# A gated mix of attention and a channel MLP: other buffers for the MLP's finished tiles, chunk sums copied in two halves, and one chunk's last half batch moved up a turn

## The chip, the cores and the metric

The kernel runs on one core of a Trainium2 chip. A core has a matrix engine (TensorE, PE in the profile, with its weight loads as PEld), a vector engine (DVE), a scalar engine (ACT), GpSimd (POOL), a sync engine (SP) that mainly issues DMAs, and sixteen DMA engines. Every engine works through its own list of instructions in order; an instruction waits until the semaphores it names are high enough, and what stands behind it on the same engine waits too.

The metric is the device time of one execution in microseconds (us), as the median of several runs. Lower is better.

## The reference

```python
x = A_x                                    # 1 x 2048 x 448, float32
g = sigmoid((x * gate_w).sum(-1, keepdims=True))
qkv = x @ wqkv                             # 16 heads of 28
p = softmax(q @ k.T * 28 ** -0.5)          # per head, 2048 x 2048
a = (p @ v) @ wo
y = layernorm(x)
b = gelu(y @ w1 + b1) @ w2 + b2            # 448 -> 1792 -> 448
return g * a + (1 - g) * b
```

All tensors are float32. The kernel splits each operand of a precise product into a high and a low part in a rounded format and adds three products of the parts; the product of probabilities and values is a plain float32 one.

## The kernel before, in words

**Stages.** The kernel has a head (the projections to q, k and v, until about 130 us), the MLP (until about 451 us) and the attention (until the end, 1082 us). Rows are worked on in four chunks of 512 (`CH`), heads in four groups of four; 16 pairs of group and chunk, `n` from 0 to 15, make up the attention.

**Row maxima.** The softmax needs the maximum of each row of scores before it can take exponentials. A cheap single product per tile gives scores good enough for that: `RowMax.one` (L207) issues one matmul into a PSUM bank and one DVE `reduce_max` (L214) that reads the bank. There are 1024 such pairs. They are spread over head, MLP and attention as filler, so DVE is busy with them nearly everywhere; two banks at a time serve them, and a matmul of this kind has to wait until DVE has read the bank.

**The MLP.** A planner (`Strips`) lays out the matmuls by estimated times and costs; it runs while the program is built, and its result is a fixed list of instructions. `Up` is one of 14 tiles of the first product for a chunk: when its sum is complete, ACT applies gelu into a buffer `h` (L355), ACT copies a rounded version to `hh` (L356), and POOL makes the low part `hl` (L363) from `h`. `h` has two buffers. `Down` is one of four tiles (128 rows) of the second product: when its sum is complete, its `close` (L393) has ACT copy it out of PSUM (L398) to a buffer, and ACT issues the DMA that stores it to `gbs` in device memory (L401). That buffer is `gb`, which has two copies in use alternately; in the last chunk alone the third and fourth tile use a buffer of `h`. The next tiles of `Up` are started by PE in the PSUM banks that `Down` tiles leave, and the last quarter of an `Up` tile is not issued before the earlier chunk's `Down` tiles are closed.

**The attention.** The work runs in turns. A turn is one pass of the loop at the end: `turn_of` (L1132) issues the score matmuls of 5, 6 or 7 units (a unit is 128 keys of one head against 512 queries, three matmuls into a bank), in two halves, and after each half one ACT exponential over the half's banks (L1170). Between them `lone` (L1119) places row maximum matmuls: three in a turn of 5 units (banks 6, 5 and 6 again), two in a turn of 6 (both in bank 6), none in a turn of 7. Then follow the functions that an agenda holds for this turn, and at the end the value matmuls: `batch` (L1175) multiplies the probabilities of four units with values, summing into bank 7 (`pv`). In a turn of 6 or 7 units a quota of three or four half batches (256 of the 512 columns) applies, so that a batch is sometimes split over two turns. After the 16th batch of a pair, `valued` (L1100) ends the pair: its sum in bank 7 is copied out (`finish_a`, L1022), and the next pair's first batch overwrites bank 7, so it waits for the copy. One column of the sum is the softmax denominator. `finish_a` sends it by DMA into a small tile, two turns later `finish_b` (L1029) takes the reciprocal on DVE, stores it to device memory (L1035) and reads it back spread over partitions (`rc`, four DMAs, L1037, which wait for the store), and four turns later `finish_c` (L1039) multiplies on POOL. DMAs of this kind all stand in SP's list.

Of the kernel before, what the change touches and what calls it, by code (L numbers as in the profile page):

```python
# [15 lines left out]
P = 128  # L16
# [3 lines left out]
DH = 28  # L20
F = 1792
NG = 4
CH = 512
NC = S // CH
NT = S // P
# [10 lines left out]
def kernel(ctx: ExitStack, tc: tile.TileContext, xt, wqk, wv, wo, xk, w1, b1, w2, b2,  # L36
                          ident_d, sel_d, out):
    nc = tc.nc
# [21 lines left out]
    rls = dram.tile([NG * NC, 4, CH], F32, name="rls")  # L60
# [101 lines left out]
    class RowMax:  # L162
# [64 lines left out]
        def close(self, n):  # L227
            mf, mt = self.mf[n % 2], self.mt[n % 2]
            nc.vector.reduce_max(mf[:, 0:16], self.mx[n % 2].rearrange("p j i k -> p (j i) k"), axis=AX)
            nc.vector.transpose(mt, mf)  # L230
# [138 lines left out]
    class Down(Piece):  # L369
# [21 lines left out]
            return st.hready.get((self.c, f, p), 1e9) > now or self.c == 0 and st.w2ready.get(f, 1e9) > now  # L391

        def close(self, st, now):  # L393
            if self.c == NC - 1 and self.i > 1:
                gb = mhp[0].tile([P, CH], F32, name="h", bufs=2)[:, :D]
            else:
                gb = mhp[0].tile([P, D], F32, name="gb", bufs=2)
            nc.scalar.activation(gb, bk[:, self.bank, :D], AF.Copy)  # L398
            st.use("act", now + 0.2, 0.56)
            st.free[self.bank] = st.act + 0.1  # L400
            nc.scalar.dma_start(gbs[self.c * TPC + self.i], gb)  # L401
            st.use("act", now, 0.5)

    class Strips:
# [28 lines left out]
        def at(self, t, fn, **uses):  # L433
            self.tasks.append((t, self.count, fn, uses))
            self.count += 1
# [457 lines left out]
    for i, key in enumerate(load):  # L893
        r = slots[i % 8]
# [48 lines left out]
    def turn_bank(i):  # L943
        return (i + shift) % 6
# [47 lines left out]
    def split_o(g, c, o):  # L992
        if c not in ohs:
            ohs[c] = ao.tile([P, NG, CH], F32R, name="oh"), ao.tile([P, NG, CH], F32R, name="ol")
        h, l = (t[:, g] for t in ohs[c])
        nc.gpsimd.tensor_copy(h, o)
        nc.gpsimd.tensor_sub(l, o, h.bitcast(F32))
# [16 lines left out]
    def project(tt):  # L1014
        po = bk[:, 6, :D]
        products(po, tt, range(NG))
        put(po, tt)

    pv = bk[:, 7]
    obs = {}  # L1020

    def finish_a(n):  # L1022
        ob = ao.tile([P, CH], F32, name="ob", bufs=1)
        lt = ao.tile([P, CH // 32], F32, name="lt")
        obs[n] = ob, lt
        nc.vector.tensor_copy(ob, pv)  # L1026
        nc.sync.dma_start(lt, ob[DH:P:32, :])

    def finish_b(n):  # L1029
        ob, lt = obs[n]  # L1030
        rc = ao.tile([P, CH], F32, name="rc", bufs=1)
        obs[n] = ob, rc
        nc.vector.reciprocal(lt, lt)
        r = rls[n]
        nc.sync.dma_start(r.rearrange("j (a b) -> (j a) b", b=CH // 32), lt)  # L1035
        for j in range(4):
            nc.sync.dma_start(rc[32 * j:32 * j + 32], r[j].partition_broadcast(32))  # L1037

    def finish_c(n):  # L1039
        g, c = divmod(n, NC)  # L1040
        ob, rc = obs.pop(n)
        if g < NG - 1:
            nc.gpsimd.tensor_mul(ot[g][:, c * CH:(c + 1) * CH], ob, rc)
            return
        nc.gpsimd.tensor_mul(ob, ob, rc)
        split_o(g, c, ob)
# [31 lines left out]
    def begun(n, turn):  # L1078

        g, c = divmod(n, NC)  # L1080
        if n + 1 < NG * NC:
            for j in range(4):
                at(turn + 1 + j // 2, lambda j=j: fetch_qq(n + 1, j))
            at(turn + 5, lambda: split_qq(n + 1))
            at(turn + 7, lambda: load_ms(n + 1))
        if c == (0 if g == 0 else 2) and g < NG - 1:
            for j in range(4):
                at(turn + 2 + j, lambda j=j: fetch_kk(g + 1, j))
                at(turn + 8 + j, lambda j=j: split_kk(g + 1, j))
            at(turn + 13, lambda: key_row(g + 1))  # L1090
            for t in range(2):
                at(turn + 9 + t, lambda t=t: load_v(g + 1, slice(8 * t, 8 * t + 8)))
        if g == NG - 1:
            for i in range(TPC):
                at(turn + 7 + i, lambda i=i: fetch_acc(c, i))
                at(turn + 9 + i // 2, lambda i=i: weigh_acc(c, i))
            for x in range(NG - 1):
                at(turn + 4 + x, lambda x=x: split_o(x, c, ot[x][:, c * CH:(c + 1) * CH]))

    def valued(n, turn):  # L1100

        g, c = divmod(n, NC)
        if n == NG * NC - 1:
            finish_last(n)
            return
        finish_a(n)
        at(turn + 2, lambda: finish_b(n))
        at(turn + 4, lambda: finish_c(n))
        if g == NG - 1:
            for i in range(TPC):  # L1110
                tail.append((turn + 6 + i, c * TPC + i))
# [7 lines left out]
    def lone(s, b, turn):  # L1119
        if not rowmax.ready(s) or turn < cold[s]:  # L1120
            return
        for kind, n, j in rowmax.one(s, bk[:, b]):
            if kind == "q":
                at(turn + 1, lambda n=n, j=j: rowmax.load_q(n, j))
            elif kind == "k":
                at(turn + 1, lambda n=n, j=j: rowmax.load_k(n, j))
                cold[j] = turn + 5
            else:
                at(turn + 1, lambda n=n: rowmax.close(n))
                at(turn + 2, lambda n=n: rowmax.store(n))  # L1130

    def turn_of(u, turn):  # L1132

        left = UNITS - u
        owed = rowmax.left()
        size = 5 if owed and owed > 2 * ((left - 104) // 6) + 6 * sixes[0] else 6
        sixes[0] = size == 6
        if not owed and not (tail and tail[0][0] <= turn + 1):
            size = 7
        size = min(left, size)  # L1140
        na = min(4 if size == 7 else 3, size)
        nb = size - na
        for x in range(u, u + size):
            n = x // 64
            if n not in begins:
                begins.add(n)
                begun(n, turn)
        extra = {5: ((0, 3, 6), (3, 1, 5), (5, 2, 6)), 6: ((0, 3, 6), (5, 2, 6))}.get(size, ())
        if size == 7:
            sevens.append(turn)  # L1150
        place = (lambda i: i) if sevens else turn_bank
        if turn in projected:
            extra = extra[1:]
        for half, first, count in ((0, 0, na), (1, na, nb)):
            for p in range(3):
                for x, o, b in extra:
                    if x == 3 * half + p:
                        lone((u + o) % 4, b if b == 6 else turn_bank(b), turn)
                for i in range(first, first + count):
                    n, k = divmod(u + i, 64)  # L1160
                    k, j = divmod(k, 4)
                    r = slice(32 * j, 32 * j + DH + (p == 0))
                    ks = slice(k * P, (k + 1) * P)
                    w = (khi, klo, khi)[p][n // NC]
                    q = (qh, qh, ql)[p][n % 3]
                    nc.tensor.matmul(bk[:, place(i)], w[r, ks], q[r], start=(p == 0), stop=(p == 2), skip_group_check=True)  # L1166
            if count:
                t = ap.tile([P, 4 - half, CH], F32, name=f"p{half}")
                b = place(first)
                nc.scalar.activation(t[:, :count], bk[:, b:b + count], AF.Exp, scale=SCALE)  # L1170
                for i in range(count):
                    prob[u + first + i] = t[:, i]
        return size

    def batch(b, turn, sl=slice(0, CH)):  # L1175
# [10 lines left out]
    begun_half = False  # L1186
    while b < UNITS // 4:
        before, quota = u, 99
        if u < UNITS:
            u += turn_of(u, turn)  # L1190
            if u - before > 5:
                quota = 3 + (before // 4 - b > 2)
        for fn in agenda.pop(turn, ()):
            fn()
        if turn == 0:
            idle(6, 7)
        if before == UNITS:
            products(bk[:, 6, :D], (NC - 1) * TPC, range(NG - 1))
            before = u = UNITS
        while 4 * b + 4 <= before and quota:  # L1200
            if quota == 1 and not begun_half:
                if b % NT:
                    batch(b, turn, slice(0, CH // 2))
                    begun_half = True
                break
            last = batch(b, turn, slice(CH // 2 if begun_half else 0, CH))
            quota -= 1 if begun_half else 2
            b, begun_half = b + 1, False
            if last:
                break  # L1210
        if tail and tail[0][0] <= turn:
            project(tail.pop(0)[1])
            projected.add(turn + 1)
        turn += 1
# [53 lines left out]
```

## Time and profile before

| | |
|---|---|
| median of 3 runs | 1082.11 us (1080.81 to 1086.48) |
| the profiled execution, its own time | 1083.55 us |
| its span, first to last instruction | 1081.8 us |
| PE busy | 1068.8 us, 99% of the span |
| DVE busy | 740.8 us, 68% |
| ACT busy | 634.0 us, 59% |
| POOL busy | 368.3 us, 34% |
| the DVE copies of a pair's sum (L1026) | 15, 691 ns each |
| ACT's copies of a finished MLP tile (L398) | 16, 545 ns each |

In the profile, a line of the timeline reads: start in us from the start of the span, duration, engine, line of the kernel, operation, what it writes and reads, how many of the same kind are merged into the row (x3), and in brackets the idle time of the engine just before, with what ended it. The four 32-row strips of PE work side by side, and so do its four 32-column groups, so that the durations of PE rows overlap. A row of windows gives, for a stretch of time, its length and then the busy time of PE, PEld, DVE, ACT and POOL in it.

### The profile page before, as it was taken

The numbers are of one execution on the slowest core, as the hardware profiler recorded it, in microseconds if no ns is written. First come the engines' busy times: TensorE is split into PE (matmuls) and PEld (weight loads), VectorE is DVE, ScalarE is ACT, GpSimd is POOL, SyncE is SP. The second block draws the span as 40 slices with busy tenths as digits, with TensorE's granted clock in tenths as the row PEclk, the third lists the DMA queues.
The fourth block names the chain that finished last, engine by engine and source line by source line (L and its number), as shares of the span: only waits on it lengthen the run. The fifth ranks groups of instructions, "written<-read, shape, count | busy, mean of one in ns | idle before, by whom it ended". The sixth has DMA issues, their size and how long they took to land.

```text
span 1081.8 us, 31072 instructions
## 1 busy us (share of the span) xinstructions
PE 1068.8 (99%) x13450; PEld 725.4 (67%) x13450; DVE 740.8 (68%) x1186; ACT 634.0 (59%) x654; POOL 368.3 (34%) x388
## 2 busy tenths in 40 slices
PE   9999999999999999999999999999999999999997
PEld 6999999999999899844444444444444444464555
DVE  4899998999999999876667655676664444422102
ACT  5234463042142033288788788778888888857671
POOL 4565577336244037441001101300110332444431
PEclk9999999999999999999999999999999999999999
DMA  6696433212100104220000011310000301011111
GB/s 232 214 269 217 168 111 104 77 46 61 45 7 7 46 12 118 92 77 18 25 11 27 16 31 38 78 41 6 25 26 23 71 27 50 25 55 36 61 47 67
DMA packets 47785, 73.20 MB, mean 68 GB/s; under 512 B 13840, under 2 KB 28816, under 8 KB 46848
## 3 DMA queue, kind: packets, MB, share of 16 engines
q1 hardware_dynamic: 33888, 39.11, 12.4%
q0 software_dynamic: 5120, 16.89, 5.5%
q10 hardware_dynamic: 8640, 15.21, 3.9%
q8 instruction: 105, 1.72, 0.7%
q14 instruction: 32, 0.26, 0.1%
HBM read 51.75 MB, written 19.31 MB: 66 GB/s over the span
## 4 chain that ended last, share of the span: by engine, by line
PE 95%; ACT 2%; DMA 2%; DVE 1%; issue 1%; SPq 0%; DVEq 0%; ACTq 0%
PE bk L488 34%; PE bk L1178 22%; PE bk L1166 18%; PE bk L212 15%; PE bk L1004 1%; ACT p L1170 1%; PE bk L1005 1%; PE bk L1006 1%; DMA gbs<-gb 1%; PE bk L920 1%; DMA first<-in_xt 1%; ACT gb L398 0%; DVE ob L1026 0%; PE bk L948 0%; DVE mx L214 0%
## 5 line engine op out<-in xcount | busy, mean ns | idle before, releaser
L214 DVE TENSOR_REDUCE mx<-bk 128x1 f32<-128x512 f32 x1024 | 673.7, 688 | 221.8 <-PE bk L212 178.6
L1170 ACT ACTIVATE p<-bk 128x1536 f32<-128x1536 f32 (+1 forms) x381 | 481.1, 1315 | 125.8 <-PE bk L1166 125.1
L212 PE MATMUL bk<-kd,qd 28*128 28x512 f32 x1024 | 449.8, 441 | 0.6 <-DVE mx L214 0.2
L212 PEld LDWEIGHTS bk<-kd,qd 28*128 28x128 f32 x1024 | 186.0, 182 | 179.7 <-DVE mx L214 115.1
L488 PE MATMUL bk<-yh,w1f 32*128 32x512 f32 x1568 | 192.9, 393 | 2.2 <-ACT gb L398 2.2
L488 PE MATMUL bk<-yl,w1f 32*128 32x512 f32 x784 | 167.4, 392 | 0.0
L488 PEld LDWEIGHTS bk<-yh,w1f 32*128 32x128 f32 x1568 | 154.6, 183 | 4.9 <-ACT gb L398 3.4
L488 PE MATMUL bk<-w2h,hh 32*128 32x448 f32 x896 | 145.0, 366 | 0.0
L488 PE MATMUL bk<-w2l,hh 32*128 32x448 f32 x896 | 144.1, 363 | 0.0
L1178 PE MATMUL bk<-p,va 128*32 128x512 f32 (+1 forms) x1144 | 130.2, 556 | 0.0
L1178 PE MATMUL bk<-p,vb 128*32 128x512 f32 (+1 forms) x1184 | 129.2, 542 | 0.0
L363 POOL TENSOR_TENSOR hl<-h,hh 128x512 fp32r<-128x512 f32 x56 | 72.4, 1305 | 137.2 <-ACT hh L356 99.7
L840 POOL CAST yh<-yl 128x512 fp32r<-128x512 f32 x16 | 9.8, 611 | 288.0 <-DMA yl<-qk 131.2
L488 PEld LDWEIGHTS bk<-yl,w1f 32*128 32x128 f32 x784 | 105.8, 183 | 0.3
L488 PEld LDWEIGHTS bk<-w2l,hh 32*128 32x128 f32 x896 | 103.1, 183 | 0.3
L488 PEld LDWEIGHTS bk<-w2h,hh 32*128 32x128 f32 x896 | 102.7, 183 | 0.4
L1166 PE MATMUL bk<-yh,ka 29*128 29x512 f32 x512 | 101.1, 483 | 0.5 <-ACT p L1170 0.5
L1166 PE MATMUL bk<-yh,kb 29*128 29x512 f32 x512 | 96.5, 480 | 1.7 <-ACT p L1170 1.7
L488 PE MATMUL bk<-w2h,hl 32*128 32x448 f32 x896 | 93.1, 362 | 0.0
L398 ACT ACTIVATE gb<-bk 128x448 f32<-128x448 f32 x14 | 7.6, 545 | 136.8 <-PE bk L488 129.7
L1166 PE MATMUL bk<-yh,la 28*128 28x512 f32 x512 | 83.4, 393 | 0.0
L488 PEld LDWEIGHTS bk<-w2h,hl 32*128 32x128 f32 x896 | 82.4, 183 | 0.3
(141 smaller groups left out, 1604.5 us busy)
## 6 DMA issues: line engine op xcount, KB each, us to landing
qk<-qo ACTq DMA_DIRECT2D x28, 256.0 KB
raw<-in_xt SPq DMA_DIRECT2D x17, 256.0 KB
vs<-vt ACTq DMA_DIRECT2D x16, 256.0 KB
rc<-rls SPq DMA_DIRECT2D x60, 64.0 KB
bxr<-in_xk POOLq DMA_DIRECT2D x8, 448.0 KB, 6.4
acc<-gbs SPq DMA_DIRECT2D x16, 224.0 KB
out_y<-acc SPq DMA_DIRECT2D x16, 224.0 KB
qd<-qk SPq DMA_DIRECT2D x60, 56.0 KB
```

Source lines behind the costliest of these rows:

```text
L212: nc.tensor.matmul(ps, self.qd[n % 2][r, i * P:(i + 1) * P], self.kd[r, k * 512:(k + 1) * 512], start=True, stop=True)
L214: nc.vector.reduce_max(self.mx[n % 2][:, j, i, k:k + 1], ps, axis=AX)
L363: nc.gpsimd.tensor_sub(hl[f], h, hh[f].bitcast(F32))
L488: mm = nc.tensor.matmul(bk[:, x.bank, :n], a, b, start=x.first, stop=(len(x.rem) == 1 and m == len(ops) - 1), skip_group_check=True)
L840: nc.gpsimd.tensor_copy(h, l.bitcast(F32))
L920: nc.tensor.matmul(bk[:, b], w, v, start=(i == 0), stop=(i == len(ops) - 1), skip_group_check=True)
L1004: nc.tensor.matmul(po, h, woh[:, g], start=(g == 0), stop=False, skip_group_check=True)
L1005: nc.tensor.matmul(po, h, wol[:, g], start=False, stop=False, skip_group_check=True)
L1006: nc.tensor.matmul(po, l, woh[:, g], start=False, stop=(g == NG - 1), skip_group_check=True)
L1166: nc.tensor.matmul(bk[:, place(i)], w[r, ks], q[r], start=(p == 0), stop=(p == 2), skip_group_check=True)
L1170: nc.scalar.activation(t[:, :count], bk[:, b:b + count], AF.Exp, scale=SCALE)
L1178: nc.tensor.matmul(bk[32 * j:32 * j + 32, 7, sl], vg[n // NC][:, k, 32 * j:32 * j + 32], prob[4 * b + j][:, sl], start=(k == 0), stop=(k = ...
```

## The change

There are four edits.

1. In `Down.close`, the third and fourth tile (`i > 1`) of every chunk use a buffer of `h`, where before only the last chunk's did.
2. `finish_a` copies the first 256 columns of bank 7 at once and leaves the other 256 columns, with the DMA that picks the denominators, in a list `late`. `copy_rest` issues what is in that list; it is called in the next turn right after the first `lone` matmul with its reduction, and at the end of `turn_of`.
3. The four DMAs that read the reciprocals back are taken out of `finish_b` into `spread_rc`, which the agenda calls one turn later.
4. In a turn with a quota, if the pair has exactly one half batch more to do than the quota, the quota is raised by one.

```diff
@@ class Down
         def close(self, st, now):
-            if self.c == NC - 1 and self.i > 1:
+            if self.i > 1:
                 gb = mhp[0].tile([P, CH], F32, name="h", bufs=2)[:, :D]
             else:
                 gb = mhp[0].tile([P, D], F32, name="gb", bufs=2)
@@
+    late = []
+
     def finish_a(n):
...
-        nc.vector.tensor_copy(ob, pv)
-        nc.sync.dma_start(lt, ob[DH:P:32, :])
+        nc.vector.tensor_copy(ob[:, :CH // 2], pv[:, :CH // 2])
+
+        def rest():
+            nc.vector.tensor_copy(ob[:, CH // 2:], pv[:, CH // 2:])
+            nc.sync.dma_start(lt, ob[DH:P:32, :])
+
+        late.append(rest)
+
+    def copy_rest():
+        while late:
+            late.pop()()
 
     def finish_b(n):
...
-        r = rls[n]
-        nc.sync.dma_start(r.rearrange("j (a b) -> (j a) b", b=CH // 32), lt)
+        nc.sync.dma_start(rls[n].rearrange("j (a b) -> (j a) b", b=CH // 32), lt)
+
+    def spread_rc(n):
         for j in range(4):
-            nc.sync.dma_start(rc[32 * j:32 * j + 32], r[j].partition_broadcast(32))
+            nc.sync.dma_start(obs[n][1][32 * j:32 * j + 32], rls[n][j].partition_broadcast(32))
@@ valued
         at(turn + 2, lambda: finish_b(n))
+        at(turn + 3, lambda: spread_rc(n))
         at(turn + 4, lambda: finish_c(n))
@@ turn_of
                         lone((u + o) % 4, b if b == 6 else turn_bank(b), turn)
+                        copy_rest()
...
+        copy_rest()
         return size
@@ the loop
                 quota = 3 + (before // 4 - b > 2)
+                quota += 2 * (NT - b % NT) - begun_half == quota + 1
```

Three places in the lists of instructions show what moves. The first is ACT's list at the end of the MLP's first chunk: the copies of `Down` tiles (L398), their stores (L401), and the first gelus of the next chunk (L355). In brackets stand the semaphores that an instruction waits for; DMAHW ones are those of DMAs.

```order
 L398 ACTIVATE gb<-bk 128x448 [waits PE_49]
 L401 DMA gbs<-gb 128x448 [waits DMAHW3_49,Activation_49]
-L398 ACTIVATE gb<-bk 128x448 [waits DMAHW2_49,PE_49]
-L401 DMA gbs<-gb 128x448 [waits DMAHW4_49,Activation_49]
-L398 ACTIVATE gb<-bk 128x448 [waits DMAHW3_49,PE_49]
-L401 DMA gbs<-gb 128x448 [waits DMAHW5_49,Activation_49]
-L355 ACTIVATE h<-bk,b1s 128x512 [waits PE_49]
+L398 ACTIVATE h<-bk 128x448 [waits PE_49]
+L401 DMA gbs<-h 128x448 [waits DMAHW4_49,Activation_49]
+L398 ACTIVATE h<-bk 128x448 [waits PE_49]
+L401 DMA gbs<-h 128x448 [waits DMAHW5_49,Activation_49]
+L355 ACTIVATE h<-bk,b1s 128x512 [waits DMAHW4_49,PE_49]
```

The third and fourth copies no longer wait for the stores of the first and second; instead the next chunk's first two gelus wait for the stores of the third and fourth.

The second is DVE's list at the end of the first pair (n = 0): `ob` is the buffer of the sum, L214 are the row maxima.

```order
-L1026 COPY ob<-bk 128x512
-L214 TENSOR_REDUCE mx_155<-bk 128x1 x6
-L1033 RECIPROCAL lt<-lt 128x16
+L1027 COPY ob<-bk 128x256
+L214 TENSOR_REDUCE mx_155<-bk 128x1
+L1030 COPY ob<-bk 128x256
+L214 TENSOR_REDUCE mx_155<-bk 128x1 x5
+L1043 RECIPROCAL lt<-lt 128x16
```

The one copy has become two with one row maximum between them.

The third is PE's list at the end of the pair n = 11. L212 are row maximum matmuls and L1166 scores (L1179 in the changed kernel); L1178 (there L1192) are the value matmuls, with `va` the values of the pair that ends and `vb` those of the next. Before:

```order
L1178 MATMUL bk<-p_14610,va 32x256 x2
L1178 MATMUL bk<-p_14623,va 32x256 x2
L212 MATMUL bk<-kd,qd_153 128x512
L1166 MATMUL bk<-yh,kb 128x512 x3
L1166 MATMUL bk<-yh,lb 128x512 x3
L1166 MATMUL bk<-yl,kb 128x512 x3
L1166 MATMUL bk<-yh,kb 128x512 x3
L1166 MATMUL bk<-yh,lb 128x512 x3
L212 MATMUL bk<-kd,qd_153 128x512
L1166 MATMUL bk<-yl,kb 128x512 x3
L1178 MATMUL bk<-p_14610,va 32x256 x2
L1178 MATMUL bk<-p_14623,va 32x256 x2
```

Now:

```order
L1192 MATMUL bk<-p_14621,va 32x512 x3
L1192 MATMUL bk<-p_14634,va 32x512 x2
L212 MATMUL bk<-kd,qd_153 128x512
L1179 MATMUL bk<-yh,kb 128x512 x3
L1179 MATMUL bk<-yh,lb 128x512 x3
L1179 MATMUL bk<-yl,kb 128x512 x3
L1179 MATMUL bk<-yh,kb 128x512 x3
L1179 MATMUL bk<-yh,lb 128x512 x3
L212 MATMUL bk<-kd,qd_153 128x512
L1179 MATMUL bk<-yl,kb 128x512 x3
L1192 MATMUL bk<-p_14634,vb 32x512
L1192 MATMUL bk<-p_14655,vb 32x512 x3
```

Before, the pair's last half batch stood alone in a turn of its own; now it goes with the batch before, and the next turn holds a whole batch of the next pair. This is the only one of the 16 pair ends at which edit 4 changes anything: PE's list is the same at all others, and the two meet again four turns later.

## The prediction

> **What bounds the kernel now.** I read the page's totals first, then its chain of work that ended last.
>
> ```profile
> PE 1068.8 (99%) x13450; PEld 725.4 (67%) x13450; DVE 740.8 (68%) x1186; ACT 634.0 (59%) x654; POOL 368.3 (34%) x388
> PE 95%; ACT 2%; DMA 2%; DVE 1%; issue 1%; SPq 0%; DVEq 0%; ACTq 0%
> ```
>
> PE sets the end nearly everywhere, and the change leaves its work as it is: one split batch fewer out of some thirty. So the time can only come from places where PE stands still. The 99% hides some of these, because four matmuls run side by side and one that runs out still counts as busy. I looked for them by windows around the ends of the MLP's chunks, and by the starts of the exponentials in the attention, which follow PE's turns.
>
> **Edit 1, the MLP's finished tiles.** First the busy times around the three chunk ends, with an undisturbed stretch between; behind the length stand PE, PEld, DVE, ACT and POOL.
>
> ```profile
> 210.00:213.00 3.00, 2.75 (x41) 2.29 (x37) 2.70 (x5) 1.23 (x3) 0.00 (x0) 1.00 0.23 81
> 291.00:294.00 3.00, 2.35 (x36) 1.88 (x35) 2.40 (x4) 0.84 (x3) 0.00 (x0) 1.00 0.42 153
> 294.00:371.00 77.00, 77.00 (x1331) 73.33 (x1328) 75.66 (x119) 21.18 (x34) 22.96 (x18) 1.00 0.05 16
> 371.00:377.00 6.00, 4.65 (x81) 4.03 (x77) 4.58 (x8) 1.64 (x3) 0.00 (x0) 1.00 0.28 97
> ```
>
> PE lacks 0.25, 0.65 and 1.35 us there, 2.25 together, and DVE 0.30, 0.60 and 1.42, together 2.32, while both are full in between (DVE 75.66 of 77). The timeline of the three ends says why.
>
> ```profile
> 211.64 0.54 ACT L398 ACTIVATE gb<-bk 128x448 f32<-128x448 f32 x1 [1.31 <-DMA gbs<-gb]
> 292.90 0.54 ACT L398 ACTIVATE gb<-bk 128x448 f32<-128x448 f32 x1 [1.71 <-DMA gbs<-gb]
> 371.88 0.33 ACTq L401 DMA_DIRECT2D gbs<-gb  x1
> 373.86 0.36 PE L488 MATMUL bk<-w2h,hl 32*128 32x448 f32 x1
> 376.03 0.54 ACT L398 ACTIVATE gb<-bk 128x448 f32<-128x448 f32 x1 [3.18 <-DMA gbs<-gb]
> 376.63 0.49 PE L488 MATMUL bk<-yh,w1f 32*128 32x512 f32 x1 [1.35 <-ACT gb L398]
> ```
>
> At the third end the tile's last matmul is over at 374.22 (373.86 and 0.36), but ACT starts the copy at 376.03, when the store issued at 371.88 has freed the buffer after 4.15 us; PE needs the bank that this copy empties and restarts at 376.63. With buffers of `h` none of the copies waits for a store of its own chunk. ACT could have begun 1.8 us earlier.
>
> What this gives: at least PE's 2.25. At most, each stall also hides what the matmuls before it took to run out: 0.39 us each (0.36 to 0.49 in these rows) while in full flow one starts every 0.058 (77 us over 1331), so 0.33 each and 3.25 in all. DVE is nearly as full as PE and stands idle in the same places for 2.32, so if it shares the pace I get no more than that. I take 2.8, between the two. Below that stands a doubt: whether the stores are late in every run. The DMA view of 372.5 to 374.6 shows a transfer of 16 KB beside the stores, of the kind that loads instructions:
>
> ```profile
> q8 instruction: 1, 0.02, 4.7%
> ```
>
> 4.7% of 16 engines over 2.1 us is 1.6 us on one engine. The store is spread over all engines and is done when the last of them is, so I take it that one piece stood behind this load. Such loads come at fixed places of a program, so I expect them to fall on the same stores again. Were none late, the third end would have no stall, and I would put the whole edit at 0.4.
>
> What it costs: the next chunk's first two gelus now wait for these stores. At the second end they are earliest:
>
> ```profile
> 295.51 0.69 ACT L355 ACTIVATE h<-bk,b1s 128x512 f32<-128x512 f32 x1 [1.06 <-PE bk L488]
> 297.48 0.69 ACT L355 ACTIVATE h<-bk,b1s 128x512 f32<-128x512 f32 x1 [0.61 <-PE bk L488]
> ```
>
> There the fourth copy would start at about 292.7 (third and fourth back to back behind 290.65, one us each) and its store be issued at 293.2; the gelu that wants its buffer comes at 297.48 less the 1 us gained, 296.5. That leaves 3.3 us. A store as late as 4.15 would hold ACT 0.85 us, and behind it the bank that this gelu empties. I take nothing for it.
>
> **Edit 2, the copy in halves.** A normal turn of 5 units, then the turn after a pair's end (n = 0); PEld rows of L212 are the first and third row maximum matmul of the turn.
>
> ```profile
> 705.17 0.18 PEld L212 LDWEIGHTS bk<-kd,qd 28*128 28x128 f32 x1 [0.84 <-DVE mx L214]
> 705.70 2.00 DVE L214 TENSOR_REDUCE mx<-bk 128x1 f32<-128x512 f32 x3 [0.72 <-PE bk L212]
> 706.45 0.18 PEld L212 LDWEIGHTS bk<-kd,qd 28*128 28x128 f32 x1 [0.19 <-DVE mx L214]
> ...
> 493.22 0.18 PEld L212 LDWEIGHTS bk<-kd,qd 28*128 28x128 f32 x1 [0.84 <-DVE mx L214]
> 493.42 0.69 DVE L1026 COPY ob<-bk 128x512 f32<-128x512 f32 x1 [0.37 <-PE bk L1178]
> 494.03 1.96 DVE L214 TENSOR_REDUCE mx<-bk 128x1 f32<-128x512 f32 x3
> 494.76 0.18 PEld L212 LDWEIGHTS bk<-kd,qd 28*128 28x128 f32 x1 [0.40 <-DVE mx L214]
> ```
>
> Normally the reduction starts 0.53 after the first matmul and the third matmul, which needs the same bank, goes at 1.28. With the copy in front the reduction starts at 0.81 and the third matmul goes at 1.54: PE loses 0.26. The exponentials show the same loss per turn:
>
> ```profile
> 494.30 2.37 ACT L1170 ACTIVATE p<-bk 128x1536 f32<-128x1536 f32 x2 [0.28 <-PE bk L1166]
> 497.27 2.37 ACT L1170 ACTIVATE p<-bk 128x1536 f32<-128x1536 f32 x2 [0.60 <-PE bk L1166]
> 500.00 1.45 ACT L1170 ACTIVATE p<-bk 128x1536 f32<-128x1536 f32 x1 [0.36 <-PE bk L1166]
> ...
> 558.78 2.36 ACT L1170 ACTIVATE p<-bk 128x1536 f32<-128x1536 f32 x2 [0.33 <-PE bk L1166]
> 562.35 2.37 ACT L1170 ACTIVATE p<-bk 128x1536 f32<-128x1536 f32 x2 [1.20 <-PE bk L1166]
> 570.54 2.36 ACT L1170 ACTIVATE p<-bk 128x1536 f32<-128x1536 f32 x2 [0.40 <-PE bk L1166]
> 574.36 2.37 ACT L1170 ACTIVATE p<-bk 128x1536 f32<-128x1536 f32 x2 [1.46 <-PE bk L1166]
> ...
> 828.59 2.79 ACT L1170 ACTIVATE p<-bk 128x1536 f32<-128x1536 f32 x2 [0.41 <-PE bk L1166]
> 831.74 2.79 ACT L1170 ACTIVATE p<-bk 128x1536 f32<-128x1536 f32 x2 [0.35 <-PE bk L1166]
> 835.14 2.79 ACT L1170 ACTIVATE p<-bk 128x1536 f32<-128x1536 f32 x2 [0.61 <-PE bk L1166]
> ```
>
> A turn of 5 units with one batch takes 2.73 and after an end 2.97; with two batches 3.57, and after an end 3.82; a turn of 6 takes 3.15, and after an end 3.40.
>
> No row has a copy of 256 columns. These two bound it:
>
> ```profile
> L1026 DVE COPY ob<-bk 128x512 f32<-128x512 f32 x15 | 10.4, 691 | 13.5 <-PE bk L1178 13.5
> L1033 DVE RECIPROCAL lt<-lt 128x16 f32<-128x16 f32 x15 | 3.7, 244 | 1.9 <-DMA lt<-ob 1.9
> ```
>
> A straight line from 16 columns (0.244) to 512 (0.691) puts 256 at 0.46; the ends are 0.345 (half) and 0.69 (no shorter at all). I take 0.46, 0.38 of it in the chain, since the reduction at 494.03 starts 0.08 before the copy is over. The first half then delays the first reduction by 0.05 instead of 0.28, and the third matmul goes at 1.33. The second half stands between the first and second reduction. The third ends at 0.58 + 2.00 + 0.38 = 2.96, and the next turn's first matmul, in the same bank, goes at 3.02: 0.3 late, where a turn of one batch ends at 2.73. So **after a turn of 5 units with one batch nothing is gained**: the wait moves from the third matmul to the next turn's first. Two batches (0.84 more) cover it.
>
> [...]
>
> By PE's list, the turn after the end has 5 units and two batches five times (0.26 less 0.05, so 0.21 each, 1.05), 5 units and one batch five times (0), 6 units twice (0.25 less 0.05, 0.4 together). The remaining three are n = 10, where ACT sets the pace (its pair of turns is under the next edit), n = 11 (next edit) and n = 14, whose turn has no row maxima: nothing. The edit gives 1.45. The next pair's first value matmul waits for the second half too: it is over at 0.58 + 0.69 + 0.38 = 1.65 after the turn's first matmul, and that value matmul comes at 1.33 + 0.43 = 1.76.
>
> **Edit 4, the last half batch**, moves work at one end, n = 11.
>
> ```profile
> 803.38 5.50 ACT L1170 ACTIVATE p<-bk 128x1536 f32<-128x1536 f32 x4 [0.34 <-PE bk L1166]
> 809.65 2.79 ACT L1170 ACTIVATE p<-bk 128x1536 f32<-128x1536 f32 x2 [0.77 <-PE bk L1166]
> ...
> 895.35 2.79 ACT L1170 ACTIVATE p<-bk 128x1536 f32<-128x1536 f32 x2 [0.42 <-PE bk L1166]
> 903.35 1.45 ACT L1170 ACTIVATE p<-bk 128x1536 f32<-128x1536 f32 x1 [0.76 <-PE bk L1178]
> 911.85 1.45 ACT L1170 ACTIVATE p<-bk 128x1536 f32<-128x1536 f32 x1 [0.77 <-PE bk L1166]
> ```
>
> Five turns of 6 units with 3, 1, 4, 3 and 4 half batches take 911.85 - 895.35 = 16.50; the one with a single half is too short for its two exponentials, and ACT falls behind. Now they hold 4, 2, 3, 3 and 3. A turn with four costs 3.57 (as above), a pair with two and three 6.27 (803.38 to 809.65, both exponentials of each turn merged in the row), two with three 6.30: 16.14. That is 0.36.
>
> **Edit 3, the reciprocals**, I put at nothing.
>
> ```profile
> SPq L1037 <- DMA rls<-lt: 16.7, 15, 2.0
> ```
>
> SP waits 1.1 us per pair for the store before it reads it back; now other DMAs (key and query loads, at four places of SP's list) may go in that gap. But no wait of PE in the attention ends on a DMA, and these loads serve a pair at least six turns away. The readers of `rc` are multiplications on POOL, 34% busy; a late one holds back POOL's splits of the next queries, which have as many turns. Without that cover, a turn's delay of the last pairs would show in the projections at the end.
>
> **Sum.** 2.8 + 1.45 + 0.36 = 4.6 us off the profiled execution's 1083.55 gives 1078.9. That execution is 1.44 above the median of the runs shown; taken off the median, 1082.11 - 4.6 = **1077.5**.
>
> **Rivals.**
>
> *Everything hides.* Halves of 0.35 us slip in between the reductions, giving 0.26 at 13 ends, and PE regains 3.25: 3.25 + 3.4 + 0.36 = 7.0, so 1075.1. For it: the gaps of 0.7 us of DVE in every normal turn (705.70). Against: those lie before the first reduction, where only the first half can use them.
>
> *The stalls of the MLP were chance.* Without late stores before, edit 1 gives 0.4, in all 2.2: 1079.9. For it: the median lies 1.44 below the profiled execution. Against: the instruction load beside the late store.
>
> *Slower: a half costs as much as a whole.* At 0.69 the first half delays the reduction as before and the second adds its 0.61 to the chain: the next turn's first matmul goes at 0.81 + 2.00 + 0.61 + 0.06 = 3.48 instead of 2.97, a loss of 0.5 at five ends, and at eight the value matmul waits until 2.2 instead of 1.97, 0.2 each: 4.1 lost, 0.36 and 2.8 gained, 1083.0. It decides against the change from about 0.65 us per half. Against: the reciprocal of 16 columns takes only 0.244. With the MLP's chance stalls as well it is 1085.4.
>
> **How the numbers follow.** Forecast 0.50, everything hides 0.22, chance stalls 0.18, slower 0.10. A measurement of this kernel can tell about 0.5%, 5.4 us, from no change; the bounds are 1076.7 and 1087.5. The forecast lies 0.8 above the lower one, and its unsure sizes (2.25 to 3.25 in the MLP, 0.39 to 0.46 per half) put about a third of it below: 0.16. With most of the first rival (0.20) that makes faster 0.36; slower is 0.04, the end of the slow case with an unlucky run (the highest shown is 1086.48); same 0.60. The range runs from 1074.6 (everything hides, half a us of scatter) to 1081.5 (chance stalls, with a share of late gelus and a scatter of 1).
>
> **What would show it.** In the profile after: no ACT copy L398 that waits for a store; PE full in the windows of the chunk ends; gelus without a wait for `gbs<-h`. [...] Turns after an end: 3.62 with two batches, 3.20 with six units, but still 2.97 or 3.0 with one. The five turns at n = 11 in 16.1. PE in the projections without waits for POOL. I am wrong if a gelu stands for a us behind a store, or if the windows are full and the time has not moved.

## The result, and the profile after

The changed kernel takes **1077.34 us** (median of 6 runs, 1075.61 to 1079.76), the kernel before on the same chips 1083.38 (6 runs, 1080.81 to 1086.48): a ratio of **0.9948, with a 95% interval of 0.9934 to 0.9962**. That ratio is worth 5.6 us (the two medians lie 6.0 apart), and the interval lies on the faster side of 1 throughout. One run of the kernel with edit 2 alone took 1658.21 us at a granted clock of 0.557 and is left out of its ratio below. The profiled execution has a span of 1076.2 us, 5.5 less than the one before. Its totals and its chain of work that ended last:

```profile
PE 1065.3 (99%) x13442; PEld 725.8 (67%) x13442; DVE 740.3 (69%) x1201; ACT 633.2 (59%) x654; POOL 367.5 (34%) x388
PE 97%; ACT 1%; issue 1%; DMA 0%; DVE 0%; DVEq 0%; SPq 0%; ACTq 0%
```

PE's share of the chain has gone from 95 to 97%; the 2% of DMA and the 1% of DVE are gone. Where the 5.5 us came from can be read off three marks that both traces have: the first copy of a finished MLP tile (L398), the first exponential, and the start of the last one.

| stretch | before | after | |
|---|---|---|---|
| start to the first L398 | 207.05 | 208.36 | +1.31 |
| from there to the first exponential | 246.20 | 242.67 | -3.53 |
| first to last exponential | 605.57 | 602.26 | -3.31 |
| from there to the end of the span | 22.9 | 22.9 | 0.0 |

The first stretch is not touched by the change; its 1.3 us are scatter (in the eight profiles of this study that share its code it took 206.5 to 210.9). The other two hold the gain. The windows around the three chunk ends of the MLP, shifted to where the ends now lie:

```profile
211.00:214.00 3.00, 3.00 (x54) 2.92 (x48) 2.99 (x5) 1.64 (x3) 0.00 (x0) 1.00 0.41 151
291.00:294.00 3.00, 3.00 (x53) 2.92 (x51) 2.91 (x5) 1.63 (x3) 0.00 (x0) 1.00 0.53 197
370.00:376.00 6.00, 6.00 (x107) 5.91 (x105) 5.92 (x10) 1.63 (x3) 0.00 (x0) 1.00 0.43 154
```

PE is full in all three, and DVE nearly. The third end on ACT's timeline:

```profile
371.49 0.33 ACTq L401 DMA_DIRECT2D gbs<-h  x1
372.49 0.33 ACTq L401 DMA_DIRECT2D gbs<-h  x1
373.84 0.55 ACT L398 ACTIVATE gb<-bk 128x448 f32<-128x448 f32 x1 [1.37 <-PE bk L488]
376.75 0.69 ACT L355 ACTIVATE h<-bk,b1s 128x512 f32<-128x512 f32 x1 [2.37 <-DMA gbs<-gb]
```

The fourth copy now waits for PE, not for a store. The two stores issued at 371.49 and 372.49 are as late as before: by the landing records of the trace they are complete after 4.20 and 3.76 us (4.07 and 3.60 before), while an undisturbed one takes 1.92 to 1.94. Nobody stands behind them any more. The next gelu, which needs the first of these buffers, free at 375.69, comes at 376.75. Its row names a store (`gbs<-gb`), but that one landed at 376.77, after the gelu had started; PE's last semaphore update before the start came at 376.73, so I put the wait down to PE.

In the attention, the half copies (groups by line: count, busy us, mean ns) and the turn after the end of the first pair, first on DVE, then the row maximum matmuls' weight loads:

```profile
L1027 DVE COPY ob<-bk 128x256 f32<-128x256 f32 x15 | 6.4, 425 | 14.7 <-PE bk L1192 14.7
L1030 DVE COPY ob<-bk 128x256 f32<-128x256 f32 x15 | 6.2, 415 | 0.0
```

```profile
491.22 0.43 DVE L1027 COPY ob<-bk 128x256 f32<-128x256 f32 x1 [0.39 <-PE bk L1192]
491.56 0.68 DVE L214 TENSOR_REDUCE mx<-bk 128x1 f32<-128x512 f32 x1
492.16 0.41 DVE L1030 COPY ob<-bk 128x256 f32<-128x256 f32 x1
492.49 1.28 DVE L214 TENSOR_REDUCE mx<-bk 128x1 f32<-128x512 f32 x2
```

```profile
491.01 0.18 PEld L212 LDWEIGHTS bk<-kd,qd 28*128 28x128 f32 x1 [0.84 <-DVE mx L214]
492.30 0.18 PEld L212 LDWEIGHTS bk<-kd,qd 28*128 28x128 f32 x1 [0.15 <-DVE mx L214]
493.82 0.18 PEld L212 LDWEIGHTS bk<-kd,qd 28*128 28x128 f32 x1 [0.92 <-DVE mx L214]
```

The first reduction starts 0.55 us after the first matmul of the turn (0.81 before), and the third matmul goes at 1.29 (1.54 before, 1.28 in a normal turn). The next turn's first matmul follows at 2.81, behind the third reduction. The first half takes 0.425 us and the second 0.415.

The exponentials show the turns after an end: 5 units with one batch, 5 units with two, and 6 units; then the five turns around the end of n = 11.

```profile
492.09 2.37 ACT L1183 ACTIVATE p<-bk 128x1536 f32<-128x1536 f32 x2 [0.29 <-PE bk L1179]
494.91 2.37 ACT L1183 ACTIVATE p<-bk 128x1536 f32<-128x1536 f32 x2 [0.46 <-PE bk L1179]
...
567.91 2.37 ACT L1183 ACTIVATE p<-bk 128x1536 f32<-128x1536 f32 x2 [0.34 <-PE bk L1179]
571.48 2.37 ACT L1183 ACTIVATE p<-bk 128x1536 f32<-128x1536 f32 x2 [1.20 <-PE bk L1179]
...
827.54 2.79 ACT L1183 ACTIVATE p<-bk 128x1536 f32<-128x1536 f32 x2 [0.34 <-PE bk L1179]
830.70 2.79 ACT L1183 ACTIVATE p<-bk 128x1536 f32<-128x1536 f32 x2 [0.37 <-PE bk L1179]
...
890.86 2.79 ACT L1183 ACTIVATE p<-bk 128x1536 f32<-128x1536 f32 x2 [0.42 <-PE bk L1179]
906.95 1.46 ACT L1183 ACTIVATE p<-bk 128x1536 f32<-128x1536 f32 x1 [0.35 <-PE bk L1179]
```

They take 2.82 (2.97 before), 3.57 (3.82) and 3.16 (3.40); the last two are as long as normal turns. The five turns take 16.09 (16.50).

### The profile page after: what moved, and what is told of

It reads as the page before. It is cut to its first block, busy times and chain, and to the rows that moved or that the text cites. A ratio compares the mean times of both kernels' runs of the same rounds, so it can differ in the third digit from the quotient of the medians.

```text
span 1076.2 us, 31074 instructions
## 1 busy us (share of the span) xinstructions
PE 1065.3 (99%) x13442; PEld 725.8 (67%) x13442; DVE 740.3 (69%) x1201; ACT 633.2 (59%) x654; POOL 367.5 (34%) x388
## 4 chain that ended last, share of the span: by engine, by line
PE 97%; ACT 1%; issue 1%; DMA 0%; DVE 0%; DVEq 0%; SPq 0%; ACTq 0%
PE bk L488 35%; PE bk L1192 22%; PE bk L1179 19%; PE bk L212 15%; PE bk L1004 1%; ACT p L1183 1%; PE bk L1005 1%; PE bk L1006 1%; PE bk L920 1%; DMA first<-in_xt 0%; PE bk L948 0%; DVE acc L1011 0%; PE bk L905 0%; PE bk L1079 0%; PE bk L1073 0%
## 5 line engine op out<-in xcount | busy, mean ns | idle before, releaser
L214 DVE TENSOR_REDUCE mx<-bk 128x1 f32<-128x512 f32 x1024 | 673.8, 688 | 215.8 <-PE bk L212 173.3
L212 PE MATMUL bk<-kd,qd 28*128 28x512 f32 x1024 | 449.4, 440 | 0.1
L212 PEld LDWEIGHTS bk<-kd,qd 28*128 28x128 f32 x1024 | 186.0, 182 | 176.6 <-DVE mx L214 117.2
L1192 PE MATMUL bk<-p,va 128*32 128x512 f32 (+1 forms) x1136 | 130.0, 559 | 0.0
L1192 PE MATMUL bk<-p,vb 128*32 128x512 f32 (+1 forms) x1184 | 129.4, 542 | 0.0
L1179 PE MATMUL bk<-yh,ka 29*128 29x512 f32 x512 | 100.6, 483 | 0.4 <-ACT p L1183 0.4
L1179 PE MATMUL bk<-yh,kb 29*128 29x512 f32 x512 | 95.9, 480 | 1.6 <-ACT p L1183 1.6
L1179 PE MATMUL bk<-yh,la 28*128 28x512 f32 x512 | 82.9, 393 | 0.0
L1179 PE MATMUL bk<-yl,ka 28*128 28x512 f32 x512 | 81.8, 407 | 0.0
```

Of the source, the lines that this page charges most:

```text
L212: nc.tensor.matmul(ps, self.qd[n % 2][r, i * P:(i + 1) * P], self.kd[r, k * 512:(k + 1) * 512], start=True, stop=True)
L214: nc.vector.reduce_max(self.mx[n % 2][:, j, i, k:k + 1], ps, axis=AX)
L1192: nc.tensor.matmul(bk[32 * j:32 * j + 32, 7, sl], vg[n // NC][:, k, 32 * j:32 * j + 32], prob[4 * b + j][:, sl], start=(k == 0), stop=(k = ...
```

## Experiments

Eight kernels ran. The attention turned out to repeat within some 0.2 us from one execution to the next where its code is the same, so stretches of the trace tell apart what totals cannot. This table has the same stretches for all of them (us, from one profiled execution each), and the ratio to the kernel before on the same chip.

| kernel | first L398 to first exponential | first to last exponential | ratio, 95% interval |
|---|---|---|---|
| before | 246.20 | 605.57 | |
| changed | 242.67 | 602.26 | 0.9948 (0.9934 to 0.9962) |
| edit 1 alone | 242.61 | 605.51 | 0.9967 (0.9955 to 0.9980) |
| edit 2 alone | 246.16 | 602.68 | 0.9975 (0.9962 to 0.9988) |
| edit 3 alone | 245.87 | 605.58 | 0.9991 (0.9981 to 1.0002) |
| edit 4 alone | 243.98 | 604.97 | 0.9982 (0.9970 to 0.9994) |
| before, shifted | 243.36 | 605.33 | 1.0089 (1.0074 to 1.0104) |
| edit 1, shifted | 243.21 | 605.36 | 1.0084 (1.0067 to 1.0101) |
| whole copy behind | 242.64 | 604.36 | 0.9962 (0.9947 to 0.9977) |
| third matmul last | 242.85 | 601.28 | 0.9955 (0.9938 to 0.9972) |

For the size of an edit the stretches are the better guide. Edits 1, 2 and 4 alone gain 3.59, 2.89 and 0.60 in the stretch that they touch, 7.1 together, and the kernel with all four gains 6.8 in the two stretches. The ratios of the four single edits add up to 9.2 us against 5.6 for all together; each has an interval of 1.1 to 1.4 us either way, and the runs don't say more about the rest.

### Edit 1 alone

```diff
-            if self.c == NC - 1 and self.i > 1:
+            if self.i > 1:
```

> Edit 1 alone on the kernel before: third and fourth MLP tile of every chunk into buffers of h. My theory: no copy L398 waits for a store any more, PE is full around the three chunk ends, and the MLP (end of the first chunk's first tile to the first exponential) is shorter by 2.3 to 3.5 us; the attention keeps its length within 0.3 us; time 0.2 to 0.35% under the kernel before. Rival, that the changed kernel's gain came from a different head or from chance: the MLP gains under 1 us.

Windows around the three ends:

```profile
210.50:213.50 3.00, 3.00 (x54) 2.83 (x48) 2.99 (x6) 1.61 (x3) 0.00 (x0) 1.00 0.42 157
290.50:293.50 3.00, 3.00 (x54) 2.73 (x47) 2.90 (x6) 1.63 (x3) 0.00 (x0) 1.00 0.58 213
370.00:376.00 6.00, 6.00 (x106) 5.79 (x102) 5.99 (x10) 1.63 (x3) 0.00 (x0) 1.00 0.35 126
```

PE is full, the MLP stretch is 3.6 us shorter, the attention unchanged to 0.06. The edit carries all of the gain in the MLP.

### Edit 2 alone

```diff
...
-        nc.vector.tensor_copy(ob, pv)
-        nc.sync.dma_start(lt, ob[DH:P:32, :])
+        nc.vector.tensor_copy(ob[:, :CH // 2], pv[:, :CH // 2])
+
+        def rest():
+            nc.vector.tensor_copy(ob[:, CH // 2:], pv[:, CH // 2:])
+            nc.sync.dma_start(lt, ob[DH:P:32, :])
+
+        late.append(rest)
...
```

> Edit 2 alone: the pair sums copied in halves. My theory: turns after a pair's end lose 0.05 or less with two batches or six units (0.26 before) and 0.1 to 0.15 with one batch, so the attention is 2.3 to 2.8 us shorter; the MLP keeps its stalls (0.25, 0.65, 1.35 us of PE). Time 0.2 to 0.25% under the kernel before. Rival, that edits 3 and 4 carried part of that: the attention gains 1.5 us or less here.

The attention is 2.89 us shorter and the MLP stretch as it was (246.16), with its stalls: PE is busy for 2.41 of 3, 2.66 of 3 and 4.61 of 6 us in windows at the ends. So 2.9 of the 3.3 us in the attention belong to the halves.

### Edit 3 alone

```diff
...
-        for j in range(4):
-            nc.sync.dma_start(rc[32 * j:32 * j + 32], r[j].partition_broadcast(32))
+
+    def spread_rc(n):
+        for j in range(4):
+            nc.sync.dma_start(obs[n][1][32 * j:32 * j + 32], rls[n][j].partition_broadcast(32))
...
+        at(turn + 3, lambda: spread_rc(n))
```

> Edit 3 alone: the four reads of the reciprocals one turn later. My theory: no turn of the attention changes by more than 0.1 us and the time stays within 0.1% of the kernel before; SP waits less than 16.7 us for the stores of the reciprocals. Rival: freeing SP's list lets other loads land earlier and gives 1 us or more, or POOL gets the factors late and the projections lose 1 us or more.

The attention takes 605.58 against 605.57, and the ratio's interval holds 1. The waits in SP's list, here in this kernel:

```profile
SPq L1038 <- DMA rls<-lt: 13.8, 14, 1.2
```

SP still waits 14 times for the store (15 times, 16.7 us, before; 17.0 in the kernel with all four edits). At most pairs nothing stands between the store and the reads in SP's list, so the reads run up to the same wait.

### Edit 4 alone

```diff
                 quota = 3 + (before // 4 - b > 2)
+                quota += 2 * (NT - b % NT) - begun_half == quota + 1
```

> Edit 4 alone: the last half batch of the pair n = 11 taken along. My theory: the five turns there take 16.1 to 16.2 us instead of 16.50, everything else is as before; time 0.03% under the kernel before, which the total cannot tell from none. Rival: the longer turn delays the next pair's start and the gain is given back within ten turns.

The exponentials at both ends of the five turns:

```profile
892.97 2.79 ACT L1170 ACTIVATE p<-bk 128x1536 f32<-128x1536 f32 x2 [0.40 <-PE bk L1166]
909.07 2.79 ACT L1170 ACTIVATE p<-bk 128x1536 f32<-128x1536 f32 x2 [0.35 <-PE bk L1166]
```

16.10 us against 16.50, and nothing of it is given back: the whole attention is 0.60 shorter. The ratio says more, 0.6 to 3.2 us. In the profiled execution 2.2 of it lie in the MLP, where this kernel has the code of before; there the second store of the third end landed after 2.30 us, not 4.07, and PE had no stall at that end. The load of instructions beside it began 1.88 us after that store was issued, in the kernel before 1.05 us after; here it held up the third store (3.23), for which no copy waits. That this was so in its other runs too isn't shown; the total of this edit stays open.

### The instruction loads shifted, without and with edit 1

64 matmuls of 64 columns, whose result nobody reads, are put at the start of PE's list.

```diff
+    for _ in range(64):
+        nc.tensor.matmul(bk[:, 7, :64], rowmax.kd[:, 0:P], rowmax.kd[:, 0:64], start=True, stop=True, skip_group_check=True)
```

> The kernel before with 64 small matmuls (64 columns, their result unused) put at the start of PE's list, so that every later load of PE's instructions comes 128 PE instructions, half its period, earlier in the work. My theory, that the late MLP stores stood behind such loads: the stores of 224 KB that were late (first at the first end, second and third at the third end) now land within 2.0 us, others are late instead, and PE's idle time around the three chunk ends falls from 2.25 us to under 1. The head is longer by about 4 us. Rival, that the stores are late for another cause (their place in the work, other DMAs): the same stores are late and PE lacks about 2.25 us again.

The windows of the three ends in the shifted kernel before, and two of the copies there that waited for a store:

```profile
221.50:224.50 3.00, 3.00 (x50) 2.53 (x42) 2.98 (x5) 1.34 (x3) 0.00 (x0) 1.00 0.42 153
302.00:305.00 3.00, 2.99 (x50) 2.40 (x48) 2.56 (x5) 1.37 (x3) 0.00 (x0) 1.00 0.50 185
381.50:387.50 6.00, 6.00 (x107) 5.86 (x104) 6.00 (x10) 1.64 (x3) 0.00 (x0) 1.00 0.35 127
```

```profile
223.81 0.54 ACT L398 ACTIVATE gb<-bk 128x448 f32<-128x448 f32 x1 [1.05 <-DMA gbs<-gb]
382.86 0.55 ACT L398 ACTIVATE gb<-bk 128x448 f32<-128x448 f32 x1 [0.67 <-DMA gbs<-gb]
```

PE lacks 0.01 us where it lacked 2.25. Landing times of the four stores at each end, in us from their issue:

| | first end | second end | third end |
|---|---|---|---|
| before | 3.94, 1.94, 1.93, 1.92 | 2.60, 2.12, 1.94, 1.92 | 1.93, 4.07, 3.60, 1.92 |
| before, shifted | 1.95, 1.94, 2.06, 2.50 | 1.94, 1.93, 2.04, 3.26 | 2.60, 1.93, 1.92, 1.93 |

With PE's list shifted by half a period of its instruction loads (128 of 256 matmuls and weight loads), other stores are late, and they are mostly ones for which nobody waits. The 64 matmuls keep PE busy for 13.9 us and make the start some 11 us longer, more than the expected 4, which is why the total is above before.

> The same 64 small matmuls with edit 1. My theory: without the collisions edit 1 is worth 0.4 us, at most 1, against the shifted kernel before. Rival, that edit 1's worth doesn't hang on the instruction loads: 2.3 to 3.5 us.

With edit 1 the shifted kernel's MLP stretch is 243.21 against 243.36, and the totals are 1091.92 and 1092.22: the edit is worth 0.15 us in the trace and 0.3 in the medians, not 3.5. Both rivals on the stores fall: what edit 1 removes is a wait for stores that stand behind loads of PE's instructions. The other traces say the same. Of the 120 stores at the three ends in the ten profiles, 47 landed more than 2.0 us after their issue; 45 of them were under way during a 16 KB load of instructions, and the other two took 2.28 and 2.36. Of the 73 on time one had such a load beside it.

### The whole copy behind the first reduction

The pair's sum is copied whole, at the place of the second half.

```diff
-        nc.vector.tensor_copy(ob[:, :CH // 2], pv[:, :CH // 2])
-
         def rest():
-            nc.vector.tensor_copy(ob[:, CH // 2:], pv[:, CH // 2:])
+            nc.vector.tensor_copy(ob, pv)
```

> The changed kernel with the pair's sum copied whole (512 columns) behind the first row maximum of the next turn, not in halves. My theory, that both the place and the size count: the first reduction starts on time, but the next pair's first value matmul waits for the copy, and the turn after an end loses 0.15 to 0.25 us with two batches or six units and 0.3 to 0.5 with one batch, 2 to 3 us more in all than the changed kernel. Rival, that moving the copy behind the reduction is what gains and the halves are not needed: turns after an end as in the changed kernel, 3.57 to 3.58 with two batches.

The turn after the end of n = 2, with two batches (PEld L1191 is the first value matmul's weight load):

```profile
566.56 2.37 ACT L1182 ACTIVATE p<-bk 128x1536 f32<-128x1536 f32 x2 [0.35 <-PE bk L1178]
566.62 0.68 DVE L1029 COPY ob<-bk 128x512 f32<-128x512 f32 x1
567.36 0.16 PEld L1191 LDWEIGHTS bk<-p,va 128*32 128x32 f32 x8 [0.41 <-DVE ob L1029]
570.29 1.45 ACT L1182 ACTIVATE p<-bk 128x1536 f32<-128x1536 f32 x1 [1.36 <-PE bk L1178]
```

The value matmul waits for the copy, and the turn takes 3.73, between 3.57 (halves) and 3.82 (whole copy in front). With one batch such turns are longer than before the change: the three turns around the end of n = 0 take 8.43 us (8.35 before, 8.19 with halves). The attention is 2.1 us longer than in the changed kernel. Against the kernel before the attention is 1.2 us shorter, of which 0.6 are edit 4's by the run of it alone: the later place alone is worth some 0.6, and the cut into halves the other 2.1.

### The third row maximum matmul behind the last scores

```diff
-        extra = {5: ((0, 3, 6), (3, 1, 5), (5, 2, 6)), 6: ((0, 3, 6), (5, 2, 6))}.get(size, ())
+        extra = {5: ((0, 3, 6), (3, 1, 5), (6, 2, 6)), 6: ((0, 3, 6), (6, 2, 6))}.get(size, ())
...
+            if half:
+                for x, o, b in extra:
+                    if x == 6:
+                        lone((u + o) % 4, b, turn)
+                        copy_rest()
```

> The changed kernel with the last row maximum matmul of each turn behind the turn's last scores and ahead of the value matmuls, not ahead of the last scores. My theory, that in every turn of 5 units PE waits 0.17 us before this matmul for the first reduction (0.19 of idle weight load in the row at 706.45): the turn of one batch falls from 2.71 us to about 2.6, where DVE's three reductions set it, with some 110 such turns, and the kernel gains 8 to 15 us. Rival, that the wait only moves to the first matmul of the next turn: no change.

A normal turn of 5 units: the first and third matmul's weight loads, then the exponentials.

```profile
706.73 0.18 PEld L212 LDWEIGHTS bk<-kd,qd 28*128 28x128 f32 x1 [0.84 <-DVE mx L214]
708.02 0.18 PEld L212 LDWEIGHTS bk<-kd,qd 28*128 28x128 f32 x1
```

```profile
705.12 2.37 ACT L1188 ACTIVATE p<-bk 128x1536 f32<-128x1536 f32 x2 [0.34 <-PE bk L1179]
707.82 2.37 ACT L1188 ACTIVATE p<-bk 128x1536 f32<-128x1536 f32 x2 [0.33 <-PE bk L1179]
```

The third matmul's wait of 0.19 us is gone, and the turn still takes 2.70. My theory missed: the idle time stood on the weight loads, and PE's matmuls were not held up by it. The rival's "no change" came out, but not for its reason, since the next first matmul waits as before (0.84). PE's own work fills this turn: its value matmuls run from 708.44 to 709.50, and the next turn's first matmul starts at 709.43, after DVE's third reduction was over at 709.27. The attention is 1.0 us shorter than in the changed kernel, the total 1077.51 against 1077.34; no version beyond the changed kernel can be told from it.

## Why the prediction was right, step by step

**The forecast**, 1077.5, met 1077.34, and 4.6 us stand against the 5.6 of the ratio. The mechanisms of the edits held in the main, but two of the terms were too small, and "nothing is gained" after one batch did not come out: the two stretches that the change touches gained 6.8 us in the profiles. That the total still met has two reasons that are luck: the median of the kernel before moved from 1082.11 to 1083.38 with more runs, and the ratio's gain is smaller than that of the stretches.

**Edit 1** was put at 2.8, between 2.25 and 3.25; it measured 3.5 to 3.6. The mechanism held in each part: copies that waited for stores, PE full without the wait, late stores that recur because instruction loads come at fixed places (they start after 9419 and 12237 of PE's instructions at the second and third end in both traces, and after 6605 and 6601 at the first). The upper bound was too low by 0.3. It counted what runs out ahead of a stall; what a stop might cost after the restart was left out of it, and no run shows where these 0.3 us come from. DVE did not share the pace in the sense feared: its idle time went with PE's.

**The cost of edit 1**, gelus behind stores, was put at nothing. In the changed kernel the buffer was free 1.1 us before the gelu that is nearest behind a late store.

**Edit 2** was put at 1.45 and measured 2.9. The step that failed is a size: the third reduction's end, "0.58 + 2.00 + 0.38 = 2.96", from which I took that a turn with one batch gains nothing. The 2.00 came from a normal turn in which the second reduction waits for its matmul; queued behind one another, reductions follow each other after 0.60 (492.49 and 1.28 for two), and the half takes 0.33 of the chain, not 0.38. The next first matmul went at 2.81, not 3.02, and over four turns around each of these five ends the kernel with edit 2 alone gained 0.15 to 0.19. Of the other seven ends, six gained 0.28 to 0.32 there and not 0.20, with the first half at 0.425 and not 0.46; in the first pair's turn it delays the first reduction by 0.02 (0.55 against 0.53), where I had 0.05. The seventh, n = 13, gained 0.18; why it is less stays open. "No gain" at n = 10, 11 and 14 held: with edit 2 alone three turns there take 9.84, 9.80 and 10.64 (9.84, 9.80 and 10.62 before). The lower size per half in the sentence on the chances, 0.39, is shown by no run: the 15 first halves took 0.425 on average and the 15 second ones 0.415.

**Edit 4**, 0.36, measured 0.41 at the five turns.

**Edit 3**, nothing, held. I had let other loads go into the gap of SP's list; at most pairs there are none, and SP's wait stayed.

**The rivals.** "Everything hides" put 7.0 on the two stretches and is nearer to their 6.8 than the forecast's 4.6, though its total, 1075.1, is further off. Its 3.25 in the MLP met 3.5, and its 3.4 and 0.36 in the attention met 3.3 in all: its condition, halves in time for the reductions, was met at six ends and in part at six. "Chance stalls" fell with the shifted kernels, with a rest: in one of four profiles with the old buffers and the old places of the loads (edit 4 alone), the third end's second store landed after 2.30 us and cost PE nothing, so how late a store is does vary with when the load begins (1.88 us after the store's issue there, 1.05 in the kernel before, where the store took 4.07). "A half costs as much as a whole" fell with 0.425.

## What to carry to other kernels

When PE is 99% busy, look for its stalls in windows a few us wide and find what the copy out of PSUM in front of them waits for; a store that is done in time elsewhere may be late at the same place in most executions (in three of the four profiles with the old buffers and the old places of the loads ACT stood idle for 3.0 to 3.2 us until one store had landed, in the fourth for 1.1 at most), and a buffer whose next user comes after that store has landed costs nothing to borrow (here 1.1 us after). A long instruction on an engine that others queue for can be better in two pieces with the awaited one between them, even where the pieces take longer together (0.84 against 0.69 us). An idle time in front of a weight load is no loss until a turn gets shorter without it (here 0.19 us of it went and the turn still took 2.70).

## What the runs showed of the hardware

At the three chunk ends a store of 224 KB by ACT took 1.91 to 1.95 us from issue until its last of sixteen pieces had landed, and up to 4.26 (in the kernel with edit 2 alone) where a 16 KB load of instructions ran at the same time; two without such a load took 2.28 and 2.36. In the stores beyond 3 us fifteen pieces had landed by 1.94 and one had not. The DMA view of the changed kernel from 372.0 to 374.2 us has such a load beside the two late stores:

```profile
q8 instruction: 1, 0.02, 4.9%
```

4.9% of 16 engines over 2.2 us is 1.7 us on one engine. The queue of this row carried 105 such loads in the changed kernel, on average one in 256 of PE's 26884 matmuls and weight loads, and 64 matmuls more at the start of PE's list moved the lateness to other stores.

In the changed kernel a DVE instruction that was already waiting in the queue started 0.08 us before the one ahead of it was over by the profile: in the turn behind the end of n = 0 the second half started at 492.16, where the reduction of 0.68 us ahead of it had started at 491.56, and the two reductions at 492.49 took 1.28 together, so that one followed the other after 0.60.
